# Two layers of linear and softmax attention: loads in four pieces, weights on GpSimd's queue, another order

## The chip, the cores and the metric

The kernel runs on one core of one Trainium2 chip. The metric is the device time of one execution in microseconds; lower is better.

## The reference

The input x has 2048 rows of 1024 features; there are 32 heads of 32 features. Two kinds of block alternate, A B A B, and both layers use the same weights. Each block adds its result to x and works on a layer norm of x. A is linear attention with a learned feature map, B is softmax attention:

```python
# A: q, k, v = split(layernorm(x) @ wqkv) by head; pq = q @ w_phi[h]; pk = k @ w_phi[h]
phi_q = concat([softmax(pq), softmax(-pq)], axis=-1)
phi_k = concat([softmax(pk), softmax(-pk)], axis=-1)
kv = einsum("bhsf,bhsd->bhfd", phi_k, v)
z  = einsum("bhsf->bhf", phi_k)
num = einsum("bhqf,bhfd->bhqd", phi_q, kv)
den = einsum("bhqf,bhf->bhq", phi_q, z)[..., None] + 1e-6
x = x + (num / den) @ wo
# B
p = softmax(einsum("bhqd,bhkd->bhqk", q, k) * Dh ** -0.5)
x = x + einsum("bhqk,bhkd->bhqd", p, v) @ wo
```

## The kernel before

x stays on the chip, transposed, as the tile xT (features by rows, bf16). The 2048 rows are handled in four chunks of 512, called c in A and qc in B. All other tiles on the chip are pieces of one large tile, the arena, so every row of the profile names it; PSUM is one tile too.

No order is written out by hand, and none follows from the program's text. The kernel first collects some 11,700 operations, each with an engine, a planned duration, a priority, the operations it depends on and the buffers it uses. `Sched.run` then plays them through engine by engine in planned time: whenever an engine is free it starts the ready operation of the lowest priority whose buffers can be placed in the arena or in PSUM. The order in which they start is the order in which the instructions are emitted, so each engine's queue is fixed by planned durations, priorities and buffers. `LAT` has an engine's planned latency and `dma` (the DMA helper) a planned issue time of 0.55 and a latency by size. Where TensorE would idle during attention, `run` adds filler products on zeros (lines 1372 and 1377).

The stages of a layer, as they follow in time:

- A, keys: `layernorm`, then `a_keys` for each chunk: products with two halves of the key weights and of the value weights (`wk_slab`, `wv_slab`, 1 MB each), exponentials (line 688), a sum and a reciprocal on VectorE (692, 695), a small copy of the reciprocals on GpSimd (706), and the products of line 721, which need the copies of four row blocks. The key and query weights are multiplied with w_phi once, by `fold_phi`, and stored in DRAM as wd_k and wd_q.
- A, queries: `a_queries` (exponentials in line 814) and `a_out` with the weights `wo_s`, loaded by `slab_turned` in seven pieces for each half (line 595).
- B: `b_k`, `b_q` and `b_v` make keys, queries and values. Weights for one group of four heads come as a 256 KB tile of class w2 through `slab` (line 584). `attention` computes scores in TensorE (1104), exponentials of three tiles at a time in ScalarE (1113) and, for some units, in VectorE (`exp_dve`, lines 1040 to 1061), and the products with the values and with ones (1145). The result is copied out by line 1161. For the denominators, four small DMAs (1191) move one row of it each, VectorE takes the reciprocal (1196), a DMA writes it to DRAM (1197, tile rd), another reads it back spread over partitions (1199), and line 1202 multiplies.
- B, output: `b_o` with 256 KB tiles of B_wo (class w2o), or `b_last` in the last layer.

During B's attention in the first layer, TensorE also does the filler work of the next layer's A: keys of chunks 0 to 2 from weights that are loaded again (class slabk). The normalised chunks are stored in DRAM (xd) and loaded again for the queries (line 1262).

All DMAs but the first two are issued on SyncE's queue, in the order that `run` found. A load through `slab` is one DMA, on which all four parts of the products depend:

```python
    def slab(cls, prio, src, n, deps=(), q="SP"):
        b, v = sb(cls, PO, n)
        o = dma(prio, lambda: (nc.sync if q == "SP" else nc.scalar).dma_start(out=v(), in_=src),
                deps, [b], q=q, kb=2 * n)
        return b, v, [o] * 4
```

Of the kernel before, what the change touches and what calls it, by code (L numbers as in the profile page):

```python
# [3 lines left out]

# [6 lines left out]
ACT = mybir.ActivationFunctionType  # L11
# [9 lines left out]
C512 = 512  # L21
# [20 lines left out]
        self.rows = ()  # L42


LAT = {"PE": 0.25, "ACT": 0.2, "DVE": 0.1, "POOL": 0.2, "SP": 2.0, "AQ": 2.0}
SWITCH = 0.1
AGAIN = 0.2
RING = 0.5
LOOK = 8


class Sched:
# [97 lines left out]
            b.at = None  # L150

    def run(self):
        engines = list(LAT)
        ready = {e: [] for e in engines}
        busy = {e: 0.0 for e in engines}
# [2 lines left out]
        n = 0  # L158
# [22 lines left out]
        while left:  # L181
            moved = False
            for e in engines:
                if busy[e] > t + 1e-9 or not ready[e]:
                    continue
                skipped = []
                pick = None
                full = e == "PE" and self.live.get("E", 0) >= FULL
                while ready[e] and len(skipped) < 400:
                    item = heapq.heappop(ready[e])  # L190
                    if full and not item[3].first:
                        full = False
                        held = [i for i in ready[e] if i[3].drain] if not item[3].drain else []
                        best = min(held, key=lambda i: i[:3], default=None)
                        if best is not None and self._alloc(best[3].bufs):
                            ready[e].remove(best)
                            heapq.heapify(ready[e])
                            heapq.heappush(ready[e], item)
                            pick = best[3]
                            break  # L200
                    if item[3].along and (mode[e] != item[3].mode or item[3].rows[0] in rows) and item[3].prio > now - DUE:
                        skipped.append(item)
                        continue
                    if item[3].prio <= todo[front] + WINDOW and self._alloc(item[3].bufs):
                        pick = item[3]
                        break
                    skipped.append(item)
                for s in skipped:
                    heapq.heappush(ready[e], s)
                if pick is None and e == "PE" and self.idle is not None and self.live.get("S", 0):  # L210

                    recent = [r for r in recent if r[1] > t - SPELL]
                    worked = sum(r[1] - max(r[0], t - SPELL) for r in recent)
                    if worked >= KEEP * SPELL:
                        pass
                    elif self.bank_used[7]:

                        if accum:
                            pick = Op("PE", MM, LAT["PE"], self.idle_acc, (), 0.0, "c", 0)
                            left += 1  # L220
                    elif not self.live.get("fil", 0):
                        pick = Op("PE", MM, LAT["PE"], self.idle, (Buf("ps", 0, "idle", [(7,)]),), 0.0, "c", 0)
                        pick.bufs[0].left = 1
                        self.queue["idle"] = [list(pick.bufs), 0]
                        assert self._alloc(pick.bufs)
                        left += 1
                if pick is None:
                    continue
                if pick.first:
                    now = pick.prio  # L230
                if e == "PE":
                    recent.append((t, t + pick.dur))
                    if pick.accum is not None:
                        accum = pick.accum
                d = pick.dur
                if pick.along and (mode[e] != pick.mode or pick.rows[0] in rows):
                    d += AGAIN
                if e == "PE":
                    rows = pick.rows
                if pick.mode is not None:  # L240
                    if mode[e] is not None and mode[e] != pick.mode:
                        d += SWITCH
                    mode[e] = pick.mode
                pick.start = t
                if pick.fn not in (self.idle, self.idle_acc):
                    started[pick.prio] = started.get(pick.prio, 0) + 1
                while front < len(todo) - 1 and started.get(todo[front], 0):
                    started[todo[front]] -= 1
                    front += 1
                busy[e] = t + d  # L250
                order.append(pick)
                left -= 1
                moved = True
                n += 1
                heapq.heappush(events, (t + d, n, pick, True))
                n += 1
                lat = pick.lat
                if e in ("SP", "AQ"):
                    ring = max(ring, t + d) + (lat - LAT[e]) * RING
                    lat = LAT[e] + ring - t - d  # L260
                heapq.heappush(events, (t + d + lat, n, pick, False))
            if moved:
                continue
            if not events:
                stuck = [(o.prio, o.eng, [(b.cls, b.at) for b in o.bufs]) for e in engines for _, _, _, o in ready[e]][:8]
                raise AssertionError(f"nothing can start at {t:.1f}: {left} left, {stuck}, live {self.live}")
            t = events[0][0]
            while events and events[0][0] <= t + 1e-9:
                _, _, o, own = heapq.heappop(events)
                if not own:  # L270
                    for b in o.bufs:
                        b.left -= 1
                        if b.left == 0:
                            self._release(b)
                for x in o.out:

                    if own != (x.eng == o.eng and x.eng not in ("SP", "AQ")):
                        continue
                    x.ndep -= 1
                    if x.ndep == 0:  # L280
                        heapq.heappush(ready[x.eng], (not (x.first or x.along), x.prio - x.ahead, x.seq, x))
# [54 lines left out]
def kernel(  # L336
# [11 lines left out]
    nc = tc.nc  # L348
# [44 lines left out]
    for j in range(4):  # L393
# [4 lines left out]
        out=rep[:].rearrange("p (x j) -> p x j", j=4),  # L398
        in_=J_bf[:].rearrange("p (j d) -> p d j", d=32)[:, 0:8, :],
# [34 lines left out]
    xd = dram_p.tile([P, 3 * PO * C512], BF16, tag="xd")  # L434
    xd_v = xd[:].rearrange("p (c o n) -> p c o n", c=3, o=PO)

    sch = Sched(ARENA, QUOTA)
    op = sch.op

# [34 lines left out]
    def dma(prio, fn, deps=(), bufs=(), q="SP", kb=256, issue=0.55):  # L474
        return op(q, issue, fn, deps, bufs, prio, lat=2.0 + kb / 200.0)
# [103 lines left out]
                [s1, rstd, q], [r_b, w_b, xb], prio))  # L579
        return xb, xv, fin  # L580

    def slab(cls, prio, src, n, deps=(), q="SP"):
        b, v = sb(cls, PO, n)
        o = dma(prio, lambda: (nc.sync if q == "SP" else nc.scalar).dma_start(out=v(), in_=src),
                deps, [b], q=q, kb=2 * n)
        return b, v, [o] * 4


    def slab_turned(cls, prio, src, n):
        b, v = sb(cls, PO, n)  # L590
        o = []
        for a in range(4):
            for lo, hi, to in ((0, P - 32 * a, 32 * a), (P - 32 * a, P, 0)):
                if hi > lo:
                    o.append(dma(prio, lambda a=a, lo=lo, hi=hi, to=to: nc.sync.dma_start(
                        out=v()[to:to + hi - lo, a::4, :], in_=src[lo:hi, a::4, :]), (), [b], kb=2 * n * (hi - lo) / 512))
        return b, v, [o] * 4

    def fold_phi(col, wd_v, prio, use_pe):
# [620 lines left out]
    def wk_slab(prio, fc, cls="slab"):  # L1220
        return slab(cls, prio, wdk_v[:, :, fc * C512:(fc + 1) * C512], C512, [store["k"][fc]])

    def wv_slab(prio, fc, q="SP", cls="slab"):
        return slab(cls, prio, A_w[:, :, 2 * D + fc * C512:2 * D + (fc + 1) * C512], C512, q=q)

    def new_kv():
# [5 lines left out]
    for layer in range(2):  # L1232
# [21 lines left out]
        if layer == 0:  # L1254
            wq_s = fold_phi(0, wdq_v, base + 15, False)
            store["q"] = [s[3] for s in wq_s]
        else:
            wq_s = [slab("slab", second - 15 + fc, wdq_v[:, :, fc * C512:(fc + 1) * C512], C512, [store["q"][fc]])
                    for fc in range(2)]
            for c in range(NC - 1):  # L1260
                x_b, x_v = sb("xn", PO, C512)
                xnA[c] = (x_b, x_v, [dma(second - 20 + 20 * c, lambda c=c, x_v=x_v: nc.sync.dma_start(
                    out=x_v(), in_=xd_v[:, c, :, :]), [xnA[c]], [x_b], kb=1024)] * 4)
        wo_s = [slab_turned("slab", second - 6 + fc, A_o[:, :, fc * C512:(fc + 1) * C512], C512) for fc in range(2)]
        bv_s = [slab("slab", second - 4 + 134 * fc, B_w[:, :, 2 * D + fc * C512:2 * D + (fc + 1) * C512], C512)
                for fc in range(2)]
# [146 lines left out]
```

## Time and profile before

| | us |
|---|---|
| time before, median of 3 runs | 2373.57 |
| lowest and highest of them | 2373.34, 2375.6 |
| the profiled execution | 2381.73 |
| its span, from the first to the last instruction | 2379.9 |

The profile shows one execution. Engines are PE (TensorE), PEld (its weight loads), DVE (VectorE), ACT (ScalarE), POOL (GpSimd) and SP (SyncE, which only issues DMAs). A group's row has the line, the engine, the operation, output and input, shapes and count, then the busy time and the mean time of one, then the engine's idle time just before these instructions and what ended it. In a row by windows, the last three numbers are the clock that TensorE was granted, the mean busy share of the 16 DMA engines and GB/s.

The stages lie as follows in the span: the first layer's A up to about 360 us, its attention to about 1290, the second layer's A to about 1500, its attention to about 2368, then the tail.

### The profile page before, as it was taken

The page shows a single profiled execution, that of the slowest core. Times are in us where ns is not written, and L with a number is a line of the kernel's source. Part 1 is how long each engine was busy: PE and PEld are TensorE (multiplying, and loading weights), DVE is VectorE, ACT ScalarE, POOL GpSimd, SP SyncE. Part 2 cuts the span into 40 slices and gives each one's busy share as a digit, 9 for nine tenths or more (in the row PEclk, how much of TensorE's full clock was granted, in tenths as well). Part 3 has the DMA queues.
Part 4 walks back from the last instruction along what each step waited for, and adds up shares of the span by engine and source line. Part 5 has one row for each costly group of instructions (what it writes and reads, how often), then busy time and mean ns, then how long its engine had stood idle before and what let it go on. Part 6 is the DMA issues. An engine that isn't in the chain of part 4 may idle for free.

```text
span 2379.9 us, 67117 instructions
## 1 busy us (share of the span) xinstructions
PE 2241.8 (94%) x29746; PEld 872.4 (37%) x29816; DVE 1669.0 (70%) x2135; ACT 2072.2 (87%) x1850; POOL 25.2 (1%) x70
## 2 busy tenths in 40 slices
PE   7999999999999999999998999999999999899998
PEld 4443343333333333333333434433333333333333
DVE  7987752345678676764764776489888988977763
ACT  5436559999999999999997555899999999999998
POOL 0000000000000000000000000000000000000000
PEclk9999999999999999999999999999999999999999
DMA  9210101122131222213323001110111101111111
GB/s 213 64 37 1 32 21 36 29 52 53 44 92 54 57 59 68 82 55 86 112 73 108 28 3 34 31 27 25 36 27 31 33 25 29 40 50 44 38 30 35
DMA packets 218092, 118.69 MB, mean 50 GB/s; under 512 B 139208, under 2 KB 208840, under 8 KB 217032
## 3 DMA queue, kind: packets, MB, share of 16 engines
q1 hardware_dynamic: 215720, 112.29, 17.6%
q8 instruction: 233, 3.82, 0.7%
q10 hardware_dynamic: 2080, 2.10, 0.3%
q14 instruction: 59, 0.48, 0.1%
HBM read 78.71 MB, written 14.14 MB: 39 GB/s over the span
## 4 chain that ended last, share of the span: by engine, by line
ACT 26%; PE 16%; issue 6%; DVE 5%; DMA 1%; SPq 0%; ACTq 0%; DVEq 0%; another core or an unknown queue 0%
ACT arena L1113 25%; PE psum L480 8%; PE psum L484 2%; PE psum L1145 2%; PE psum L1104 2%; DVE arena L1058 2%; DVE arena L1061 1%; DMA arena<-rd 1%; DVE arena L1047 1%; DVE arena L1050 0%; ACT arena L688 0%; DVE arena L1202 0%; PE psum L857 0%; PE psum L1377 0%; DVE arena L1161 0%
## 5 line engine op out<-in xcount | busy, mean ns | idle before, releaser
L1113 ACT ACTIVATE arena<-psum 128x1536 bf16<-128x1536 f32 x1295 | 1749.4, 1670 | 20.5 <-PE psum L1104 12.9
L1145 PE MATMUL psum<-arena 128*32 128x512 bf16 x4096 | 626.7, 386 | 12.1 <-DVE arena L1161 7.6
L1145 PE MATMUL psum<-arena,ones_bf 128*32 128x512 bf16 x4096 | 626.6, 386 | 1.3 <-issue 1.3
L484 PE MATMUL psum<-arena 128*32 128x512 bf16 (+1 forms) x9792 | 590.0, 356 | 6.5 <-DVE arena L920 3.0
L1104 PE MATMUL psum<-arena 32*128 32x512 bf16 x3884 | 513.9, 384 | 84.0 <-ACT arena L1113 75.0
L480 PE MATMUL psum<-arena 128*128 128x512 bf16 (+1 forms) x1969 | 446.6, 376 | 10.8 <-DVE arena L1182 3.6
L1058 DVE SCALAR_TENSOR_TENSOR arena<-arena 128x1024 f32<-128x1024 f32 x318 | 387.7, 1219 | 6.3 <-PE psum L1145 2.2
L1104 PEld LDWEIGHTS <-arena 32*128 32x128 bf16 x3884 | 173.7, 91 | 572.5 <-issue 561.4
L484 PEld LDWEIGHTS <-arena 128*32 128x32 bf16 x9792 | 221.6, 96 | 231.0 <-issue 120.0
L480 PEld LDWEIGHTS <-arena 128*128 128x128 bf16 x2032 | 190.6, 98 | 245.6 <-issue 45.9
L1145 PEld LDWEIGHTS <-arena 128*32 128x32 bf16 x4096 | 166.8, 95 | 247.1 <-issue 191.1
L1047 DVE TENSOR_SCALAR arena<-psum 128x512 int32<-128x512 f32 x212 | 145.8, 688 | 80.4 <-PE psum L1040 69.6
L920 DVE CAST arena<-psum 128x512 bf16<-128x512 f32 x120 | 82.5, 687 | 155.7 <-PE psum L484 141.7
L1145 PEld LDWEIGHTS <-ones_bf 128*32 128x32 bf16 x4096 | 163.8, 95 | 30.3 <-issue 15.9
L1061 DVE SCALAR_TENSOR_TENSOR arena<-arena 128x1024 bf16<-128x1024 f32 x106 | 129.3, 1220 | 3.5 <-PE psum L1145 0.2
L688 ACT ACTIVATE arena<-psum 128x512 bf16<-128x512 f32 x80 | 43.0, 597 | 87.5 <-PE psum L480 66.6
L1161 DVE COPY arena<-psum 128x512 f32<-128x512 f32 x126 | 86.4, 686 | 44.1 <-PE psum L1145 43.0
L1377 PE MATMUL psum<-xT,zero 128*32 128x512 bf16 x1360 | 111.5, 384 | 0.0
L1202 DVE TENSOR_TENSOR arena<-arena 64x512 bf16<-64x512 f32 x124 | 84.7, 683 | 34.4 <-DMA arena<-rd 21.0
L692 DVE TENSOR_REDUCE arena<-arena 128x32 f32<-128x1024 bf16 x64 | 77.7, 1214 | 32.5 <-ACT arena L688 31.0
L814 ACT ACTIVATE arena<-psum 128x512 bf16<-128x512 f32 x128 | 69.4, 597 | 31.4 <-PE psum L480 30.6
L572 DVE TENSOR_TENSOR arena<-xT,arena 128x1024 f32<-128x1024 bf16 x64 | 77.8, 1219 | 24.4 <-ACT arena L561 23.8
(102 smaller groups left out, 1359.4 us busy)
## 6 DMA issues: line engine op xcount, KB each, us to landing
arena<-rd SPq DMA_DIRECT2D x62, 256.0 KB
arena<-in_B_wqkv_dram SPq DMA_DIRECT2D x48, 256.0 KB
arena<-in_A_wqkv_dram SPq DMA_DIRECT2D x10, 1024.0 KB
arena<-arena SPq DMA_DIRECT2D x256, 32.0 KB
arena<-in_B_wo_dram SPq DMA_DIRECT2D x32, 256.0 KB
arena<-wd_k SPq DMA_DIRECT2D x8, 1024.0 KB
arena<-arena SPq DMA_DIRECT2D x96, 64.0 KB
arena<-in_B_wqkv_dram SPq DMA_DIRECT2D x4, 1024.0 KB
```

The source lines that it names most:

```text
L480: nc.tensor.matmul(out_, lhsT=lhsT, rhs=rhs, start=start, stop=stop, skip_group_check=True)
L484: nc.tensor.matmul(out_[ks, :], lhsT=lhsT[:, ks], rhs=rhs, start=start, stop=stop, tile_position=(0, 32 * k), skip_group_check=True)
L920: return op("DVE", dve_us(512), lambda: nc.vector.tensor_copy(out=dst(), in_=src()), [dep], bufs, prio)
L1047: ys.append(op("DVE", dve_us(512), lambda k=k, s_v=s_v: nc.vector.tensor_scalar(out=y_v()[:, k, :].bitcast(I32), in0=s_v(), scalar1=POW2_B ...
L1058: last = [op("DVE", dve_us(1024), lambda i=i, c=c: nc.vector.scalar_tensor_tensor(out=x_v(), in0=(x_v() if i else m_v()), scalar=c, in1=m_ ...
L1061: eo = op("DVE", dve_us(1024), lambda: nc.vector.scalar_tensor_tensor(out=e_v(), in0=x_v(), scalar=POW2_0, in1=y_v(), op0=ALU.add, op1=ALU ...
L1104: nc.tensor.matmul(out=s_v()[:, x * C512:(x + 1) * C512], lhsT=kT[g][1]()[r, pp, d * P:(d + 1) * P], rhs=q_of[(qc, g)][1]()[r, (pp + j // ...
L1113: ex = op("ACT", act_us(w * C512), lambda s_v=s_v, e_v=e_v, w=w: nc.scalar.activation(out=e_v()[:, 0:w * C512], in_=s_v(), func=ACT.Exp, s ...
L1145: nc.tensor.matmul(out=a_v()[col:col + 32, :], lhsT=v_v()[:, kc % 4, o:o + DH] if what == 0 else ones_bf[:], rhs=ev()[:, x * C512:(x + 1) ...
L1161: cp = op("DVE", dve_us(512), lambda t_v=t_v, a_v=a_v: nc.vector.tensor_copy(out=t_v(), in_=a_v()), [last], [a_b, t_b], prio - 4)
L1202: s = [op("DVE", dve_us(512), lambda a=a, k=k, o_v=o_v, r_v=r_v, T=T: nc.vector.tensor_tensor(out=o_v()[a, :], in0=T[k][1]()[a, :], in1=r_ ...
L1377: nc.tensor.matmul(psum[32 * k:32 * k + 32, 6 * C512:7 * C512], lhsT=zero[:], rhs=xT[:, 0, 0:C512], start=False, stop=False, tile_position ...
```

## The change

- Loads of slabs that are 512 columns wide become four DMAs of 256 KB, one for each pair of row blocks; each of the four parts of the products depends on its own piece.
- `slab` takes GpSimd's queue for priorities over 100 and SyncE's below; this is nearly everything after the start. The pieces of A_wo (`slab_turned`) and the stored chunks from xd are moved to GpSimd's queue too, the latter in four pieces. DMAs within the chip, the denominators and all stores stay on SyncE.
- The planner knows the new queue as GQ, with a latency of 2.5 where SyncE has 2.0, as a queue apart from GpSimd's own work; the instructions of both stand on the same engine.
- Planned durations on VectorE and TensorE are multiplied by a random factor within 1%, from a fixed seed. This alters no instruction, only the order that the planner finds and the places of buffers.

```diff
-LAT = {"PE": 0.25, "ACT": 0.2, "DVE": 0.1, "POOL": 0.2, "SP": 2.0, "AQ": 2.0}
+LAT = {"PE": 0.25, "ACT": 0.2, "DVE": 0.1, "POOL": 0.2, "SP": 2.0, "AQ": 2.0, "GQ": 2.5}
+TIE = 14
...
     def run(self):
+        draw = random.Random(TIE)
+        for o in self.ops:
+            if TIE and o.eng in ("DVE", "PE"):
+                o.dur *= 1 + draw.uniform(-0.01, 0.01)
...
-                if e in ("SP", "AQ"):
+                if e in ("SP", "AQ", "GQ"):
...
+    ENG = {"SP": nc.sync, "AQ": nc.scalar, "GQ": nc.gpsimd}
...
-    def slab(cls, prio, src, n, deps=(), q="SP"):
+    def slab(cls, prio, src, n, deps=(), q=None):
+        q = q or ("GQ" if prio > 100 else "SP")
         b, v = sb(cls, PO, n)
-        o = dma(prio, lambda: (nc.sync if q == "SP" else nc.scalar).dma_start(out=v(), in_=src),
-                deps, [b], q=q, kb=2 * n)
-        return b, v, [o] * 4
+        if n < C512:
+            o = dma(prio, lambda: ENG[q].dma_start(out=v(), in_=src),
+                    deps, [b], q=q, kb=2 * n)
+            return b, v, [o] * 4
+        return b, v, [dma(prio + 0.001 * i, lambda i=i: ENG[q].dma_start(
+            out=v()[:, 2 * i:2 * i + 2, :], in_=src[:, 2 * i:2 * i + 2, :]),
+            deps, [b], q=q, kb=n / 2) for i in range(4)]
...
-                    o.append(dma(prio, lambda a=a, lo=lo, hi=hi, to=to: nc.sync.dma_start(
-                        out=v()[to:to + hi - lo, a::4, :], in_=src[lo:hi, a::4, :]), (), [b], kb=2 * n * (hi - lo) / 512))
+                    o.append(dma(prio, lambda a=a, lo=lo, hi=hi, to=to: nc.gpsimd.dma_start(
+                        out=v()[to:to + hi - lo, a::4, :], in_=src[lo:hi, a::4, :]), (), [b], q="GQ", kb=2 * n * (hi - lo) / 512))
...
-    def wv_slab(prio, fc, q="SP", cls="slab"):
+    def wv_slab(prio, fc, q=None, cls="slab"):
...
-                xnA[c] = (x_b, x_v, [dma(second - 20 + 20 * c, lambda c=c, x_v=x_v: nc.sync.dma_start(
-                    out=x_v(), in_=xd_v[:, c, :, :]), [xnA[c]], [x_b], kb=1024)] * 4)
+                xnA[c] = (x_b, x_v, [dma(second - 20 + 20 * c + 0.001 * i, lambda c=c, x_v=x_v, i=i: nc.gpsimd.dma_start(
+                    out=x_v()[:, 2 * i:2 * i + 2, :], in_=xd_v[:, c, 2 * i:2 * i + 2, :]),
+                    [xnA[c]], [x_b], q="GQ", kb=256) for i in range(4)])
```

More of the change, by code (lines that the diff above doesn't have):

```diff
@@ L2 @@
 import math
+import random
 from contextlib import ExitStack
@@ L275, in run @@
                 for x in o.out:
-                    if own != (x.eng == o.eng and x.eng not in ("SP", "AQ")):
+                    if own != (x.eng == o.eng and x.eng not in ("SP", "AQ", "GQ")):
                         continue
```

## The prediction

> **What bounds the kernel now.** I read the page first, then the windows cut at the stages, then ScalarE's groups inside the stages, then the short windows around the places where ScalarE loses time.
>
> ```profile
> span 2379.9 us, 67117 instructions
> PE 2241.8 (94%) x29746; PEld 872.4 (37%) x29816; DVE 1669.0 (70%) x2135; ACT 2072.2 (87%) x1850; POOL 25.2 (1%) x70
> L1113 ACT ACTIVATE arena<-psum 128x1536 bf16<-128x1536 f32 x1295 | 1749.4, 1670 | 20.5 <-PE psum L1104 12.9
> L1377 PE MATMUL psum<-xT,zero 128*32 128x512 bf16 x1360 | 111.5, 384 | 0.0
> ```
>
> ```profile
> 30.00:360.00 330.00, 323.30 (x2821) 142.03 (x2859) 255.02 (x324) 166.78 (x276) 10.40 (x32) 1.00 0.20 47
> 360.00:1009.00 649.00, 617.47 (x9340) 229.92 (x9336) 391.59 (x495) 647.99 (x496) 3.60 (x8) 1.00 0.21 57
> 1009.00:1290.00 281.00, 255.38 (x3878) 91.27 (x3877) 167.55 (x215) 262.80 (x216) 7.91 (x16) 0.96 0.29 86
> 1290.00:1500.00 210.00, 207.35 (x1547) 88.88 (x1570) 152.78 (x211) 116.38 (x200) 2.60 (x8) 0.99 0.09 26
> 1500.00:2368.00 868.00, 814.92 (x12016) 305.71 (x12017) 678.75 (x836) 859.99 (x644) 0.00 (x0) 0.99 0.12 33
> ```
>
> The columns after each window are its length and the busy time of TensorE, weight loads, VectorE, ScalarE and GpSimd, then the granted clock, the DMA share and GB/s. The two linear stages (30 to 360, 1290 to 1500) are TensorE's: 6.7 and 2.65 us idle. The two attention stages are ScalarE's: 1.0 us idle up to 1009, 8.0 us in all of the second, but 18.2 us in 1009:1290, where the next layer's keys are made beside the exponentials. The 1295 exponentials are not touched by the change; its whole room in attention is their idle time, 20.5 us, and where that lies is seen in the same groups by stage:
>
> ```profile
> L1113 ACT ACTIVATE arena<-psum 128x1536 bf16<-128x1536 f32 x181 | 246.8, 1556 | 13.1 <-PE psum L1104 8.4 <-PE psum L484 3.7 <-PE psum L1145 0.8
> L1113 ACT ACTIVATE arena<-psum 128x1536 bf16<-128x1536 f32 x637 | 857.2, 1666 | 6.7 <-PE psum L1104 4.3 <-PE psum L1145 1.7 <-PE psum L1040 0.5
> L484 PEld LDWEIGHTS <-arena 128*32 128x32 bf16 x9792 | 221.6, 96 | 231.0 <-issue 120.0 <-DMA arena<-in_B_wqkv_dram 0.8 <-DVE arena L576 0.3
> ```
>
> The first is 1009:1290, the second 1500:2368; one exponential takes 246.8/181 = 1.36 us of ScalarE. The third, over the whole span, says that loads are on time: filler products wait 0.8 us for one. So the change cannot win by bringing weights sooner; it can win where loads disturb others.
>
> ```profile
> 1090.00:1092.00 2.00, 2.00 (x131) 1.24 (x123) 0.41 (x1) 2.00 (x3) 0.00 (x0) 1.00 1.05 354
> 1094.00:1096.00 2.00, 0.58 (x8) 0.13 (x7) 0.00 (x0) 0.76 (x1) 0.00 (x0) 0.87 0.00 0
> 1096.00:1098.00 2.00, 2.00 (x22) 0.56 (x19) 0.00 (x0) 0.88 (x1) 0.00 (x0) 0.50 0.03 9
> 1098.00:1100.00 2.00, 2.00 (x27) 0.44 (x19) 0.00 (x0) 1.28 (x2) 0.00 (x0) 0.78 0.45 130
> 1172.00:1174.00 2.00, 2.00 (x39) 0.83 (x27) 1.71 (x4) 2.00 (x3) 0.00 (x0) 1.00 1.02 324
> 1180.00:1182.00 2.00, 2.00 (x23) 0.56 (x19) 1.72 (x2) 0.34 (x1) 0.00 (x0) 0.50 0.00 0
> 1182.00:1184.00 2.00, 2.00 (x23) 0.56 (x19) 0.73 (x1) 0.00 (x0) 0.00 (x0) 0.50 0.00 0
> ```
>
> Twice the DMA engines are full (354 and 324 GB/s), TensorE runs dry, the granted clock falls to 0.50, and ScalarE loses 1.24 + 1.12 + 0.72 = 3.1 us and 1.66 + 2.00 = 3.7 us. That is 6.8 us behind two bursts of loads.
>
> **The change, part by part.** The page's issues say what moves:
>
> ```profile
> arena<-in_B_wqkv_dram SPq DMA_DIRECT2D x48, 256.0 KB
> arena<-in_A_wqkv_dram SPq DMA_DIRECT2D x10, 1024.0 KB
> arena<-in_B_wo_dram SPq DMA_DIRECT2D x32, 256.0 KB
> arena<-wd_k SPq DMA_DIRECT2D x8, 1024.0 KB
> ```
>
> In the changed kernel's instruction order 210 loads stand on GpSimd's queue: 78 of these 256 KB loads (two stay), 92 quarters of 1 MB slabs, 28 pieces of A_wo, 12 quarters of the stored chunks. GpSimd has not issued one DMA so far, so the cost c of one issue there is unknown and carries the forecast. Its nearest rows:
>
> ```profile
> L584 SPq DMA_DIRECT2D arena<-in_B_wqkv_dram x52: 367/524/2646, 112.4 to 2258.3; - x52
> L584 SPq DMA_DIRECT2D arena<-in_B_wo_dram x34: 367/390/611, 580.1 to 2077.3; - x34
> L706 POOL CAST arena<-arena x64: 322/326/1097, 38.6 to 1332.8; 128x32 bf16<-128x32 f32 x64
> L1050 DVE TENSOR_SCALAR arena<-arena x106: 628/693/696, 451.9 to 2296.9; 128x1024 int32<-128x1024 int32 x106
> ```
>
> Minimum, median and maximum in ns: SyncE takes 0.37 us at best for such an issue, 2.65 at worst. I take c = 0.8, twice the median of 0.39 and nearer to the low end, since most rows lie there; 0.37 and 2.65 stay for the range.
>
> *Bursts.* A quarter lets the first pair of products start, and the planner places each quarter by itself, so three quarters of what now arrives in one go lies behind what the consumer waits for. I book three quarters of the 6.8 us: -5.1 us; bounds 0 (the same bytes over the same engines) and -6.8.
>
> *SyncE without the loads.* At the end of the first attention the denominators stand behind loads:
>
> ```profile
> 1257.86 0.57 SPq L584
> 1258.48 0.58 SPq L595
> 1259.10 0.47 SPq L595
> 1259.62 0.45 SPq L595
> 1260.23 4.59 DMA rd<-arena
> 1264.89 4.68 DMA arena<-rd
> 1260.00:1280.00 20.00, 17.55 (x227) 5.62 (x219) 8.11 (x11) 17.31 (x14) 0.00 (x0) 0.91 0.40 101
> ```
>
> In the chain four load issues hold SyncE for 1260.23 - 1257.86 = 2.4 us before the denominators leave, and their way out takes 4.59 us beside the loads. ScalarE loses 20 - 17.31 = 2.7 us in that window. I book all of it, -2.7 us, since the delay in front of it is 2.4 us plus a slow transfer; bounds 0 and -2.7. Elsewhere in attention these round trips have cover (1.0 us idle up to 1009).
>
> *GpSimd's copies behind loads.* The casts of line 706 stay on GpSimd, which takes its instructions in order. In the linear stage of layer 2 the order is: 12 stored quarters, cast, 4 A_wo pieces, cast, 3 pieces, cast, 4 quarters of B_w, cast; the fourth cast releases the line 721 products.
>
> ```profile
> 1312.04 0.33 POOL L706 CAST arena<-arena 128x32 bf16<-128x32 f32 x1 [79.13 <-DVE arena L695]
> 1320.51 0.33 POOL L706 CAST arena<-arena 128x32 bf16<-128x32 f32 x1 [2.47 <-DVE arena L695]
> 1322.03 1.20 PE L721 MATMUL psum<-arena 128*32 128x33 bf16 x128
> 1291.93 22.03 SPq L595 DMA_DIRECT2D arena<-in_A_wo_dram  x7
> L1262 SPq DMA_DIRECT2D arena<-xd x3: 319/345/345, 1280.6 to 1291.5; - x3
> 1300.86 2.04 ACT L814 ACTIVATE arena<-psum 128x512 bf16<-128x512 f32 x4
> ```
>
> The seven A_wo issues end late now (1313.96), held by a buffer, so I let none slip ahead of the first cast. Between that cast's end (1312.37) and 1322.03, less three casts of 0.33, there are 8.7 us for 11 issues: 0.79 us each. At c = 0.8 the stall is +0.1 us; at 0.37 nothing; at 2.65 it is 11 x 2.65 - 8.7 = +20.5 us, all of it on TensorE, which bounds this stage. The stored chunks have cover: the first is issued at 1280.6, and the exponentials of the queries that read it begin at 1300.86; at c = 0.8 its four quarters take 3.2 us. Booked at nothing; without the cover it would be those 3.2 us.
>
> *Loads with short leads.* At the end of the first attention 20 issues (8 slab quarters, 5 pieces of B_wo, 7 of A_wo) fall within 13 exponentials, and the last piece is wanted 20 exponentials after the first issue: 20 x 1.36 = 27 us, less 3 to land, my estimate (the loaded transfer above took 4.59). Late by 20c - 24: nothing at 0.8, +29 us at 2.65.
>
> *Start.* The value slabs stay on SyncE in eight pieces, six issues more at some 0.52 us = 3.1 us, ahead of the later transposes of x. TensorE's 323.3 of 330 us there hides it; without that cover it costs up to 3.1 us.
>
> *Layout.* Planned durations of TensorE and VectorE work are jittered by 1%, which reorders everything a little; the changed order has 1252 filler products of line 1377 in place of 1360. They run where ScalarE bounds, so their 108 x 111.5/1360 = 9 us are worth nothing by themselves.
>
> Sum: -5.1 - 2.7 + 0.1 = -7.7 us. The profiled execution took 2381.73 us with its span of 2379.9; it becomes 2374.0. It lies 8.2 us over the median of the three runs, 2373.57, which becomes **2365.9**. Anything within 0.2% (4.7 us) could not be told from no change.
>
> A page speaks against the change. The Trainium skill, "SBUF — State Buffer", section "SBUF: two separate sides", says that GpSimd builds its DMA descriptors through a port pair that VectorE can lock for a whole instruction, and advises the other queues. The trace agrees that something like it exists: one cast of line 706 took 1097 ns where the median is 326, and line 1050 handles its 1024 elements in 693 ns. What that gives is a rival.
>
> **The rivals.** *GpSimd as a queue is too slow (slower).* Each issue waits for a VectorE instruction like line 1050's: c = 0.8 + 0.69 = 1.5. Then the casts come 11 x 1.5 - 8.7 = 7.8 us late, the short leads 20 x 1.5 - 24 = 6 us, together with the gains +6.1: 2379.7. It decides from 11c - 8.7 + 20c - 24 = 7.8, c = 1.31, on; at c = 1.9 the sum is +18.4: 2392. For it: loads and casts share one in-order queue, and VectorE is 0.73 busy in 1290:1500. Against it: the cast's median of 326 ns says that GpSimd is seldom kept. That rule is the one from the page above.
>
> *The same engines (no change).* Bursts and clock dips stay, as the bytes and the engines are the same; only the 2.7 us at the layer's end are won: 2370.9. For it: the bursts ran at 354 GB/s, and no queue adds engines. The Trainium skill, "DMA: Bandwidth & Descriptors", section "Issuing engines are not separate DMA queues", says just that: spreading issues saves sequencer time only.
>
> *Another layout, other dips.* Idle before exponentials is 20.5 us in this layout. If the new one has no dips, 2353; if it has half as many again, +10 us with the gains lost: 2384.
>
> **How the numbers follow.** The forecast, faster by 3 to 12 us: 0.40. No dips: 0.08. The same engines: 0.14. GpSimd too slow: 0.28. Worse layout: 0.10. So faster 0.48, same 0.14, slower 0.38. The range runs from 2353 (all 20.5 us won) to 2392 (c = 1.9); the forecast's own is 2361 to 2370.
>
> **What would show it.** Right: in 1009:1290 and at the layer's end fewer windows at clock 0.50, idle before the exponentials near 13 us in place of 20.5, GpSimd's issue rows near 0.8 us, no TensorE wait for line 706. Wrong: TensorE waits for loads from B_wo or A_wo or for the casts in 1290:1500, or exponentials idle as long as now at other places.

## The result, and the profile after

The changed kernel took 2370.45 us (median of 20 runs, 2367.14 to 2373.21) where the kernel before took 2375.39 (20 runs, 2369.76 to 2381.11). The ratio is 0.9979, 95% interval 0.9973 to 0.9985: 4.9 us faster, 3.6 to 6.4. The middle of that lies just beyond 0.2%, its lower end does not.

The two profiled executions differ by more, 2381.73 against 2367.78 us. Each lies near an end of its kernel's runs: before's is above the 20 runs given here, after's is near the lowest of them. So the traces name the places, and the size comes from the ratio. The page of the changed kernel:

```profile
span 2365.9 us, 67269 instructions
PE 2220.7 (94%) x29629; PEld 862.9 (36%) x29696; DVE 1671.0 (71%) x2135; ACT 2068.5 (87%) x1850; POOL 184.7 (8%) x280
q1 hardware_dynamic: 105848, 60.38, 9.7%
q0 software_dynamic: 16032, 51.92, 7.5%
L1125 ACT ACTIVATE arena<-psum 128x1536 bf16<-128x1536 f32 x1295 | 1748.3, 1703 | 14.4 <-PE psum L1116 6.0
```

Line 1125 is the exponential that was line 1113, and 1116 the scores that were 1104. Its busy time is what it was (1748.3 against 1749.4 us); its idle time fell from 20.5 to 14.4. The windows cut at the same stages, and the exponentials' groups in the second part of the first attention and in the second attention:

```profile
30.00:360.00 330.00, 323.43 (x2836) 141.49 (x2872) 255.33 (x324) 167.50 (x277) 26.16 (x55) 1.00 0.19 47
1009.00:1279.00 270.00, 244.85 (x3824) 88.12 (x3822) 166.49 (x212) 261.65 (x216) 61.38 (x90) 0.99 0.29 90
1279.00:1489.00 210.00, 206.82 (x1551) 88.41 (x1572) 154.66 (x212) 116.25 (x201) 16.80 (x30) 0.99 0.09 26
```

```profile
L1125 ACT ACTIVATE arena<-psum 128x1536 bf16<-128x1536 f32 x181 | 247.8, 1617 | 4.9 <-PE psum L1116 3.8 <-PE psum L1157 0.9
```

```profile
L1125 ACT ACTIVATE arena<-psum 128x1536 bf16<-128x1536 f32 x637 | 856.9, 1701 | 8.0 <-issue 2.9 <-PE psum L1157 2.7 <-PE psum L1116 2.2
```

The stretch that was 281 us long is 270 with the same 216 instructions on ScalarE, and the 181 exponentials in it wait 4.9 us in place of 13.1. The linear stages did not move. The second attention waits 1.3 us more (8.0 against 6.7).

Where the time went is seen in 100 us around the two bursts and in the last 28 us before the last exponential of the first attention. Before:

```profile
1090.00:1190.00 100.00, 91.00 (x1329) 31.75 (x1325) 61.51 (x76) 93.14 (x76) 1.41 (x4) 0.95 0.34 101
1256.00:1284.00 28.00, 24.89 (x324) 8.02 (x317) 9.69 (x14) 25.31 (x20) 0.00 (x0) 0.94 0.43 114
```

After:

```profile
1080.00:1180.00 100.00, 91.62 (x1392) 32.09 (x1388) 64.69 (x79) 99.24 (x79) 23.98 (x34) 1.00 0.33 105
1174.00:1176.00 2.00, 2.00 (x39) 0.75 (x31) 1.02 (x2) 2.00 (x4) 0.46 (x1) 1.00 1.05 332
1245.00:1273.00 28.00, 24.37 (x324) 8.05 (x322) 11.03 (x16) 24.95 (x19) 9.21 (x15) 0.94 0.47 134
```

ScalarE's loss around the bursts falls from 100 - 93.14 = 6.9 to 0.8 us. The bursts themselves are still there (332 GB/s, the engines full), but TensorE's clock no longer falls around them: it is 1.00 throughout, where before it was 0.95 in the mean, with stretches at 0.50. At the layer's end nothing was won: 2.7 us lost before, 28 - 24.95 = 3.05 after.

As far as the profile shows, no load ended TensorE's pauses at the two bursts of before. These are the longest at each, in its timelines:

```profile
1095.41 0.57 PE L1145 MATMUL psum<-arena 128*32 128x512 bf16 x1 [2.46 <-issue]
1176.36 0.39 PE L1104 MATMUL psum<-arena 32*128 32x512 bf16 x3 [0.95 <-ACT arena L1113]
```

The first has no releaser in the profile. It lies inside a group of line 1145, right behind the 128 short products of line 721; what held TensorE there stays open. In the second, scores wait for ScalarE to free their place. Nor does the clock fall only at bursts. In the second attention before has a dip while the DMA engines rest, and the changed kernel has one behind a burst of loads in quarters:

```profile
1700.00:1702.00 2.00, 2.00 (x23) 0.46 (x19) 1.97 (x3) 1.54 (x2) 0.00 (x0) 0.50 0.01 1
2067.00:2069.00 2.00, 2.00 (x23) 0.57 (x19) 1.97 (x3) 1.20 (x1) 0.00 (x0) 0.50 0.00 0
```

### The profile page after: what moved, and what is told of

The parts are those of the page before. It is cut to its first block, busy times and chain, and to the rows that moved or that the text cites. A ratio compares the mean times of both kernels' runs of the same rounds, so it can differ in the third digit from the quotient of the medians.

```text
span 2365.9 us, 67269 instructions
## 1 busy us (share of the span) xinstructions
PE 2220.7 (94%) x29629; PEld 862.9 (36%) x29696; DVE 1671.0 (71%) x2135; ACT 2068.5 (87%) x1850; POOL 184.7 (8%) x280
## 3 DMA queue, kind: packets, MB, share of 16 engines
q1 hardware_dynamic: 105848, 60.38, 9.7%
q0 software_dynamic: 16032, 51.92, 7.5%
## 5 line engine op out<-in xcount | busy, mean ns | idle before, releaser
L1125 ACT ACTIVATE arena<-psum 128x1536 bf16<-128x1536 f32 x1295 | 1748.3, 1703 | 14.4 <-PE psum L1116 6.0
L593 POOL DMA_DIRECT2D arena<-in_B_wqkv_dram x46 | 41.1, 896 | 1167.7 <-PE psum L491 279.4
L1390 PE MATMUL psum<-xT,zero 128*32 128x512 bf16 x1252 | 102.4, 383 | 0.0
```

The lines of the kernel that those rows point to most:

```text
L1125: ex = op("ACT", act_us(w * C512), lambda s_v=s_v, e_v=e_v, w=w: nc.scalar.activation(out=e_v()[:, 0:w * C512], in_=s_v(), func=ACT.Exp, s ...
L1390: nc.tensor.matmul(psum[32 * k:32 * k + 32, 6 * C512:7 * C512], lhsT=zero[:], rhs=xT[:, 0, 0:C512], start=False, stop=False, tile_position ...
```

## The experiments

The change has three parts: quarters, GpSimd's queue, and another order. My theory: the quarters win, by keeping TensorE from running dry behind a whole 1 MB load, and the queue matters little. Rivals: the queue wins, because SyncE is freed; or the order alone wins, and the edits nothing. All ratios are against the kernel before on the same chip. Each run also records the mean clock that TensorE was granted over it. The clock column gives the mean over a kernel's runs, and behind the stroke that of the kernel before in the same series; the last column is the exponentials' idle time in the one profiled execution.

| kernel | order (seed) | loads | queue | ratio, 95% interval | clock | idle, us |
|---|---|---|---|---|---|---|
| changed | 14 | quarters | GpSimd | 0.9979 [0.9973, 0.9985] | 0.9946 / - | 14.4 |
| e1 | 14 | quarters | SyncE | 0.9987 [0.9979, 0.9996] | 0.9935 / 0.9927 | 15.5 |
| e9 | 14 | eighths | GpSimd | 0.9982 [0.9973, 0.9991] | 0.9940 / 0.9926 | 18.9 |
| e8 | 14 | whole | GpSimd | 1.0002 [0.9993, 1.0010] | 0.9926 / 0.9926 | 24.2 |
| e2 | before's | whole | GpSimd | 1.0049 [1.0035, 1.0064] | 0.9902 / 0.9927 | 19.9 |
| e5 | none | quarters | SyncE | 0.9982 [0.9973, 0.9990] | 0.9949 / 0.9927 | 13.9 |
| e7, seed 1 | 1 | quarters | SyncE | 1.0002 [0.9994, 1.0011] | 0.9944 / 0.9926 | 24.2 |
| e7, seed 2 | 2 | quarters | SyncE | 1.0001 [0.9991, 1.0010] | 0.9943 / 0.9926 | 21.0 |
| e3 | none | quarters | GpSimd | 1.0027 [1.0015, 1.0038] | 0.9928 / 0.9927 | 21.0 |
| e6, seed 1 | 1 | quarters | GpSimd | 1.0015 [1.0002, 1.0029] | 0.9935 / 0.9919 | 24.8 |
| e6, seed 2 | 2 | quarters | GpSimd | 1.0016 [1.0000, 1.0031] | 0.9926 / 0.9919 | 21.7 |
| e4, seed 1 | 1 | whole | SyncE | 1.0012 [0.9999, 1.0026] | 0.9940 / 0.9919 | 22.0 |
| e4, seed 2 | 2 | whole | SyncE | 0.9992 [0.9979, 1.0006] | 0.9942 / 0.9919 | 19.5 |

Rows of one seed share an order only among the first four: pieces or a queue that the planner knows of change its plan too.

**The queue alone, in both orders.** e1 is the changed kernel, its order included, with every load issued by SyncE:

```diff
-    ENG = {"SP": nc.sync, "AQ": nc.scalar, "GQ": nc.gpsimd}
+    ENG = {"SP": nc.sync, "AQ": nc.scalar, "GQ": nc.sync}
...
-                    o.append(dma(prio, lambda a=a, lo=lo, hi=hi, to=to: nc.gpsimd.dma_start(
+                    o.append(dma(prio, lambda a=a, lo=lo, hi=hi, to=to: nc.sync.dma_start(
```

(the stored chunks likewise). e2 is the kernel before, its order and whole loads kept, with the same loads issued by GpSimd:

```diff
-        o = dma(prio, lambda: (nc.sync if q == "SP" else nc.scalar).dma_start(out=v(), in_=src),
+        o = dma(prio, lambda: (nc.gpsimd if prio > 100 else nc.sync).dma_start(out=v(), in_=src),
```

(A_wo's pieces and the stored chunks likewise).

> The changed kernel's order on every engine, with its quarters and pieces, but all loads issued by SyncE instead of GpSimd. Theory (the gain is GpSimd's queue: SyncE freed, bursts broken): the first attention gets its idle back, ratio 1.000 to 1.003 against the kernel before, SyncE holding denominators again at the layer's end. Rival (the gain is the new order and the quarters): ratio stays near 0.998, within 2 us of the changed kernel.

> The order of the kernel before on every engine, loads whole as before, but the loads with priorities over 100, the pieces of A_wo and the stored chunks issued by GpSimd. Theory (queue): 0.997 to 0.999, a gain of 2.4 to 7 us. Rival (order and quarters): 0.999 to 1.001; if GpSimd's issues of 1024 runs cost over 1.3 us each, over 1.001.

e1 keeps the gain, at 0.9987; its interval overlaps the changed kernel's, so GpSimd's queue is worth 0.08% here or nothing. e2 loses 0.49% by its ratio; its median of 6 runs, 2385.91 us (2381.73 to 2394.78), lies 10.5 us above 2375.39. Its profiled execution was its fastest run, so its trace does not show most of the loss: its exponentials wait 19.9 us, no longer than before's.

Its runs' clocks say something: 0.9902 in the mean, the lowest of all. In each kernel the runs with a lower mean clock tend to be the longer ones (in 94 runs of the kernel before the correlation is -0.75, with 1.6 us for each 0.001; in e2's six runs -0.85 and 1.9). By 1.6 to 1.9 us, the 0.0025 that e2 lies below before account for 4 to 5 of its 10.5 us. That is a correlation, and the rest stays open. The rival "the queue wins" is out: by itself it wins nothing that can be told in the new order, and loses in the old one.

**Quarters or whole loads, in the same order.** e8 keeps the changed kernel's order and queue, and issues each 1 MB slab and stored chunk as one DMA where its first quarter stood; e9 cuts every load on GpSimd's queue in two (420 issues in place of 210).

```diff
-        return b, v, [dma(prio + 0.001 * i, lambda i=i: ENG[q].dma_start(
-            out=v()[:, 2 * i:2 * i + 2, :], in_=src[:, 2 * i:2 * i + 2, :]),
+        left = [1]
+        def part(i):
...
+            elif left:
+                left.pop()
+                ENG[q].dma_start(out=v(), in_=src)
+        return b, v, [dma(prio + 0.001 * i, lambda i=i: part(i),
```

```diff
+        def part(i):
...
+            for x in (2 * i, 2 * i + 1):
+                ENG[q].dma_start(out=v()[:, x:x + 1, :], in_=src[:, x:x + 1, :])
```

> The changed kernel with its order on TensorE, VectorE and ScalarE, but GpSimd loads each 1 MB slab and stored chunk whole where its first quarter stood; 78 issues fewer. Theory (quarters bring the gain): 0.9995 to 1.002. Rival (the order brings it): 0.997 to 0.999.

> The changed kernel with every load on GpSimd cut in two, 420 issues in place of 210: an issue's share of that queue grows from 0.5 to 0.9 us for each part to about twice that for a load. By the prediction's terms with c near 1.4 (0.7 twice): the casts 11 x 1.4 - 8.7 = 6.7 us late and the short leads 20 x 1.4 - 24 = 4 us: ratio 1.001 to 1.004. Rival (the queue has room, its loads have long leads): within 0.1% of the changed kernel, 0.997 to 0.999.

Whole loads lose the gain (1.0002), and a dip comes back near where the first burst was. The rows are from the timelines of GpSimd, SyncE, VectorE and TensorE of e8, and from its windows:

```profile
1079.04 0.88 POOL L603 DMA_DIRECT2D arena<-in_A_wqkv_dram  x1 [7.58 <-PE psum L1164]
1080.62 0.33 SPq L1216 DMA_DIRECT2D rd<-arena  x1
1085.08 0.58 SPq L1218 DMA_DIRECT2D arena<-rd  x1
1090.17 1.39 DVE L1221 TENSOR_TENSOR arena<-arena 64x512 bf16<-64x512 f32 x2 [4.39 <-DMA arena<-rd]
1091.59 1.23 DVE L720 TENSOR_TENSOR arena<-psum,arena 128x1024 bf16<-128x1024 f32 x1
1092.87 1.04 PE L491 MATMUL psum<-arena 128*32 128x512 bf16 x8 [2.70 <-DVE arena L720]
```

```profile
1090.00:1092.00 2.00, 0.17 (x4) 0.00 (x0) 1.78 (x3) 0.36 (x1) 0.00 (x0) 1.00 0.93 281
1092.00:1094.00 2.00, 1.13 (x11) 0.24 (x10) 0.82 (x1) 2.00 (x2) 0.00 (x0) 0.55 0.67 236
1094.00:1096.00 2.00, 2.00 (x19) 0.45 (x16) 0.00 (x0) 1.87 (x2) 0.00 (x0) 0.50 0.00 0
```

TensorE stands still for 2.70 us because VectorE is late with line 720, and VectorE is late because it waited 4.39 us for the denominators that are read back. Their way out to DRAM, 8 KB, was issued at 1080.62 beside the whole 1 MB load of 1079.04; the read back could be issued only 4.46 us later. The load of wd_k that fills the windows from 1090 on was issued at 1088.30 and took 5.9 us to land, so it came after TensorE had gone on at 1092.87: it did not release it. ScalarE, which waits for the same multiplication, loses 1.64 us in the window at 1090; the clock then falls to 0.50. The Trainium skill, "TensorE: Matmul & The Clock Gate", section "What's actually happening", says that the clock halves after an idle window of some 3.4 us; the two levels agree with these rows, while here 2.70 us of standing still were enough.

In the changed kernel the quarters of the same load are issued from 1072.89 to 1077.08, ahead of the denominators. Their way out takes 1.93 us, VectorE waits 2.04 us, TensorE 0.36 us, and the clock stays at 1.00:

```profile
1077.94 0.33 SPq L1209 DMA_DIRECT2D rd<-arena  x1
1079.87 0.58 SPq L1211 DMA_DIRECT2D arena<-rd  x1
1085.14 1.39 DVE L1214 TENSOR_TENSOR arena<-arena 64x512 bf16<-64x512 f32 x2 [2.04 <-DMA arena<-rd]
1087.84 0.62 PE L491 MATMUL psum<-arena 128*32 128x512 bf16 x8 [0.36 <-DVE arena L713]
```

In the second attention both kernels have a longer pause of the same kind, beside a burst of loads (over 300 GB/s), where VectorE waits for the small DMAs that move the denominators' rows. It is shorter with quarters; first e8, then the changed kernel:

```profile
2075.61 0.25 DVE L1215 RECIPROCAL arena<-arena 128x16 f32<-128x16 f32 x1 [5.52 <-DMA arena<-arena]
2076.46 0.58 PE L1059 MATMUL psum<-arena 32*128 32x512 bf16 x1 [4.53 <-DVE arena L1066]
2064.61 0.25 DVE L1208 RECIPROCAL arena<-arena 128x16 f32<-128x16 f32 x1 [3.77 <-DMA arena<-arena]
2065.46 0.37 PE L1052 MATMUL psum<-arena 32*128 32x512 bf16 x1 [2.78 <-DVE arena L1059]
```

This is one execution of each kernel; that these two places make up the difference between their times is not shown. The mean clocks over all runs go the same way: 0.9946, 0.9940 and 0.9935 with pieces, 0.9926 with whole loads. So in this order, on GpSimd's queue, the quarters are worth about 0.2%. On SyncE's queue they keep most of the gain (e1), but whole loads on that queue were not run in this order. As e2, with whole loads on GpSimd's queue, loses in the old order too, a part of e8's loss can come from that pairing; this stays open.

Twice the issues cost nothing that can be measured in the time (0.9982). GpSimd's groups in e9, and the place in TensorE's timeline of its second linear stage where they do cost:

```profile
L598 POOL DMA_DIRECT2D arena<-in_B_wqkv_dram x92 | 70.1, 767 | 1138.0 <-PE psum L491 335.2 <-issue 188.4 <-ACT arena L1135 141.5
L606 POOL DMA_DIRECT2D arena<-wd_k x64 | 35.2, 557 | 20.2 <-PE psum L491 13.6 <-ACT arena L1135 3.8 <-PE psum L1167 1.2
1319.12 1.09 PE L743 MATMUL psum<-arena 128*32 128x33 bf16 x116 [2.39 <-POOL arena L728]
```

Two issues of 0.767 us take 1.53 us for what one load of the changed kernel takes 0.896. For most loads the cost is 1.1 to 1.5 us. TensorE waits 2.39 us for the fourth cast there (line 728, line 706 in the kernel before), 0.1% of the time, which the ratio cannot tell.

**Do quarters, or the change, win in any order?** e3 is the changed kernel without the jitter, e6 with other seeds. e5 has only the quarters, planned and issued on SyncE and without jitter, e7 the same with seeds. e4 is the kernel before with jittered planning alone.

```diff
-TIE = 14
+TIE = 0
```

```diff
-        q = q or ("GQ" if prio > 100 else "SP")
+        q = q or "SP"
```

The first is e3 (1 and 2 in e6); e5 has both, with the other loads' queues put back too. e4 adds only the lines with `TIE` to the kernel before.

> The changed kernel without the random 1% on planned durations. Theory (queue and quarters give the gain): within 0.1% of the changed kernel, 0.997 to 0.999. Rival (the gain is this one layout, by luck): 1.000 or above.

> Loads in four pieces planned and issued on SyncE, no jitter: only the quarters are left of the change. Theory (queue): 1.000 to 1.003, since 87 more issues stand on SyncE. Rival (quarters break the bursts): 0.998.

> The kernel before with the random 1% on planned durations alone (seed 1; seed 14 finds no complete plan there): whole loads on SyncE, another order. Theory (quarters give the gain): 0.999 to 1.003, as an order by itself brings nothing. Rival (any of these orders is better than the one before): 0.998.

> As the one before it, with seed 2. Theory: 0.999 to 1.003. Rival: 0.998. The distance between the two says how far an order alone moves the time; I expect 2 to 6 us.

> The changed kernel with seed 1 in place of 14. Theory (quarters gain, GpSimd's queue costs, the seed decides the sign): 0.999 to 1.004, nearer to the one without jitter (1.0027) than to the changed kernel (0.9979). Rival (the change gains with any order): 0.997 to 0.999.

> The changed kernel with seed 2. Theory: 0.999 to 1.004. Rival: 0.997 to 0.999.

> Loads in four pieces on SyncE, none on GpSimd, with the jitter of seed 1. Theory (quarters on SyncE gain with any order): 0.997 to 0.999, as without jitter (0.9982). Rival (that order was a lucky one too): 1.000 to 1.003.

> The same with seed 2. Theory: 0.997 to 0.999. Rival: 1.000 to 1.003. With the run before it and the one without jitter, three orders of loads in pieces on SyncE stand against three of the changed kernel's kind (1.0027, 1.0015, 1.0016).

After e3 (slower by 0.27%) and e5 (faster by 0.18% with nothing on GpSimd) I held that the quarters win in any order. e7 refutes it: 1.0002 and 1.0001. e6 refutes that the change as a whole does: both seeds are some 0.15% slower. Whole loads under two jittered orders differ by 0.2% from each other (e4). The exponentials take the same time in all of them (1750.2 us in e5, 1748.2 in e7 with seed 1); the traces differ in how long they wait (13.9 and 24.2 us). The three kernels with under 16 us of idle time are the changed one, e1 and e5, and all are faster. The column is no measure by itself, as e9's 18.9 at 0.9982 shows. Nor is the clock: e7's and e4's is as high as e9's, without a gain, so an order also costs time in which TensorE is not slowed. What in an order decides was not found. No version beats the changed kernel; e5 equals it within the intervals, without GpSimd's queue and without jitter.

## Why the prediction was right or wrong

It said faster by 7.7 us, in a range of 2353 to 2392; measured are 4.9 us, 3.6 to 6.4. The sign holds. The largest term came out near its size, but not for the reason that I gave; the second term did not come at all, and the order was taken too lightly.

*Bursts, -5.1: the size holds, the reason does not.* Around the bursts the loss fell by 6.9 - 0.8 = 6.1 us, near my bound of 6.8. But before's profiled execution had a mean clock of 0.989, where its runs have 0.992 to 0.993 in the mean: it held more dips than most. From e8 to the changed kernel, that is for quarters instead of whole loads on GpSimd's queue, the ratio moves by 0.0023 or 5.5 us. The rival "the same engines" expected the dips to stay; at these two places they went. My reason was that a quarter lets the first pair of products start, so that the rest "lies behind what the consumer waits for". After the start of the kernel, TensorE's products wait for a load once in the whole of before (us in all, times, longest):

```profile
PE psum L484 <- DMA arena<-in_B_wqkv_dram: 0.3, 1, 0.3
```

My own row for the weight loads, 0.8 us, had said the same. What the traces show in its place is e8's chain: a large load delays the small DMAs of the denominators, VectorE waits for them, and TensorE for VectorE. Before's own two dips at the bursts did not begin in this way, so how the change removed them stays open. That the term came out near its size is luck, as far as this reason goes.

*SyncE freed, -2.7: wrong.* SyncE was freed. Its timeline at the layer's end in the changed kernel has no load between the denominators' way out and the read back:

```profile
1250.71 0.32 SPq L1209 DMA_DIRECT2D rd<-arena  x1
1253.82 0.58 SPq L1211 DMA_DIRECT2D arena<-rd  x1
```

VectorE's timeline has the reciprocal in front of the trip and the multiplication behind it, first before, then after:

```profile
1258.93 0.25 DVE L1196 RECIPROCAL arena<-arena 128x16 f32<-128x16 f32 x1 [0.45 <-DMA arena<-arena]
1269.67 1.41 DVE L1202 TENSOR_TENSOR arena<-arena 64x512 bf16<-64x512 f32 x2 [4.37 <-DMA arena<-rd]
1250.43 0.25 DVE L1208 RECIPROCAL arena<-arena 128x16 f32<-128x16 f32 x1 [1.37 <-DMA arena<-arena]
1259.06 1.40 DVE L1214 TENSOR_TENSOR arena<-arena 64x512 bf16<-64x512 f32 x2 [4.13 <-DMA arena<-rd]
```

The four loads held SyncE from 1257.86 on, but the denominators were ready only at 1258.93 + 0.25 = 1259.18 and left at 1260.23: of the 2.4 us that I counted, the loads cost 1.05. From the reciprocal's end to the landed read back, before took 1259.18 to 1269.57, 10.4 us; after takes 1250.68 to 1259.04, 8.4 us. Yet VectorE waits as long as before, 4.13 us against 4.37, TensorE 2.71 us behind it (at 1261.24; 1.79 before, at 1271.92), its clock falls there as it did before (0.94 in the mean of the 28 us in both), and ScalarE loses 2.11 + 0.94 = 3.05 us. ScalarE's timelines, after and before:

```profile
1262.87 1.45 ACT L1125 ACTIVATE arena<-psum 128x1536 bf16<-128x1536 f32 x1 [2.11 <-PE psum L1116]
1265.26 8.16 ACT L1125 ACTIVATE arena<-psum 128x1536 bf16<-128x1536 f32 x6 [0.94 <-PE psum L1157]
1276.62 8.16 ACT L1113 ACTIVATE arena<-psum 128x1536 bf16<-128x1536 f32 x6 [0.97 <-PE psum L1104]
```

The last exponential ends at 1265.26 + 8.16 = 1273.42 after, at 1276.62 + 8.16 = 1284.78 before. So the trip starts 1273.42 - 1250.68 = 22.7 us before that end, where it started 1284.78 - 1259.18 = 25.6 us before it: it is 2.0 us shorter and starts 2.9 us later. In e1 SyncE issues five loads inside this trip. VectorE waits 4.04 us and TensorE 2.63, but the clock stays at 1.00, and the last 28 us lose less, 1.7 us:

```profile
1247.00:1275.00 28.00, 23.97 (x340) 8.20 (x334) 11.16 (x16) 26.27 (x20) 0.00 (x0) 1.00 0.55 149
```

The step that failed is "I book all of it": I took a delay on the chain as the time it costs, counted in it time in which the denominators were not ready, and did not ask where the new order would put the multiplication.

*The cost of an issue on GpSimd, c = 0.8: right.*

```profile
L593 POOL DMA_DIRECT2D arena<-in_B_wqkv_dram x46: 882/882/1278, 267.2 to 2242.4; - x46
```

```profile
L607 POOL DMA_DIRECT2D arena<-in_A_wo_dram x28: 543/623/838, 96.5 to 1304.8; - x28
```

Minimum and median are equal or close (704 and 722 ns for the quarters of wd_k), so nothing keeps these issues as a rule, while VectorE is 71% busy. The rule of the Trainium skill, "SBUF — State Buffer", section "SBUF: two separate sides", that VectorE can hold off GpSimd's descriptors, is not seen in them; at most it is in the longest, 1278 ns.

*Casts behind loads, +0.1: right.* GpSimd's timeline in the second linear stage, and TensorE's at the products that need the four casts:

```profile
1300.45 0.32 POOL L718 CAST arena<-arena 128x32 bf16<-128x32 f32 x1 [15.44 <-ACT arena L700]
1301.07 2.51 POOL L607 DMA_DIRECT2D arena<-in_A_wo_dram  x4 [0.29 <-PE psum L487]
...
1306.55 2.89 POOL L596 DMA_DIRECT2D arena<-in_B_wqkv_dram  x4 [0.18 <-issue]
1309.45 0.34 POOL L718 CAST arena<-arena 128x32 bf16<-128x32 f32 x1
1310.41 1.20 PE L733 MATMUL psum<-arena 128*32 128x33 bf16 x128
```

The fourth cast ends 1309.79 - 1300.77 = 9.0 us after the first, with 11 issues of 7.2 us in all in between, inside the 9.7 us that the order of before left. The products of line 733 (line 721 before) wait for nothing, and TensorE is busy 206.82 of the stage's 210 us (207.35 before).

*"GpSimd as a queue is too slow": fell, since c stayed below its 1.31.* e9 is the nearest test of its prices. The 11 loads between the casts are 7 pieces of A_wo at 2 x 0.53 and 4 quarters at 2 x 0.55 us there, so 11c - 8.7 becomes 3.1; TensorE waits 2.39 us. The 20 loads with short leads take 23.6 us with e9's prices, within the 24 that they have. So the price for the casts holds nearly, and e9's expectation of 1.001 to 1.004 was too high because it put c at 1.4 for all of them.

*Layout worth nothing: wrong as a statement, harmless as a term.* It had two rivals, with 2353 and 2384; the seeds show 0.9992 to 1.0012 with nothing but jitter, and 0.9979 to 1.0016 among jittered orders of the changed kernel. That is as large as the whole effect, and deserved more than the 0.18 of chance that the two had together. So the sign is in part luck: the same edits are 0.27% slower without jitter and 0.15% slower with two other seeds, and nothing in the prediction told these orders apart.

## What to carry to other kernels

Where small DMAs that an engine waits for in order stand beside loads of 1 MB, the loads can be cut; with one order kept fixed, on GpSimd's queue, that was worth 0.2% here. Look up which engine ended a pause before you name its cause: the bursts of loads stood beside TensorE's pauses, but where e8's trace names a cause, TensorE waited for VectorE, and VectorE for the denominators. Where a planner makes the order, run an edit in the old order and under several seeds before crediting it: orders alone differed by 0.2%, and the same edits gave 0.9979 to 1.0027. Moving loads to another queue won nothing that could be told by itself, and a shorter chain wins only if what needs it does not come earlier too.

## What the runs showed of the hardware

- GpSimd's issue cost follows the form of the load: 0.90 us for a 256 KB tile of B's weights, 0.72 for a quarter of a slab, 0.54 to 0.56 for half a quarter in e9, and 0.54 for a quarter of a stored chunk, which has 256 KB too.
- The bytes went in other packets: the 51.92 MB on GpSimd's queue took 16032 packets (7.5% of the engines' time), while the same order on SyncE's queue (e1) took 112.30 MB in 218264:

```profile
q1 hardware_dynamic: 218264, 112.30, 17.8%
```

Less the 105848 packets and 60.38 MB that stayed, these loads were 112416 packets on SyncE's queue, seven times as many, for some 8.1% of the engines' time.
- The denominators' way out to DRAM, 8 KB, took 4.46 us up to the issue of the read back beside a 1 MB load (e8), and 1.93 us behind that load's quarters (changed kernel).
- TensorE's clock fell to 0.50 in e8 at a pause of 2.70 us, and stayed low for over 4 us while it was busy. The length of one pause did not decide it: in e1 a pause of 2.63 us at 1264.04 left it at 1.00, and in e8 it was at 0.50 from 1148 on, though no pause in the 9 us before was longer than 0.40 us.
- Runs of one kernel differ by some 3 to 9 us either way, and the longer ones tend to have the lower mean clock: a single profiled execution can lie at either end.
